# Sigmoid attention with a bilinear feed-forward: later start of the first group, thinner decoding, alternating banks for w3 and w_out

## The chip, the core and the metric

The kernel runs on one core of a Trainium2 chip. The metric is the device time of one execution in microseconds, as the median over several runs. The engines are named as in the profile: TensorE (PE, with PEld for its weight loads), VectorE (DVE), ScalarE (ACT), GpSimd (POOL) and SyncE (SP). SP and POOL here issue DMAs.

## What is computed

```python
def _attn_ref(q, k, v):                       # 8 batches, 12 heads, 448 tokens, head size 64
    scores = scale * np.matmul(q, k.transpose(0, 1, 3, 2)) - np.log(S)
    attn = 1.0 / (1.0 + np.exp(-scores))
    return np.matmul(attn, v).astype(np.float32)

def _moe_ref(x, w1, w2, w3, w_out):           # x: 3584 x 768, from the attention's output
    a = x @ w1                                # 768 x 1024
    b = x @ w2
    h = a * b @ w3                            # 1024 x 1024
    return (h @ w_out).astype(np.float32)     # 1024 x 768
```

The four weight matrices come as float64. The kernel gets them as pairs of 32-bit words and decodes them itself.

## The kernel before

**Arithmetic.** Every float32 operand of a large product is split into a high part (a cast to fp32r, mostly on ScalarE) and a low part (the operand minus its high part, on VectorE), and a product takes three matmuls: high x high, high x low, low x high. The large products are done by Strassen's method in Winograd's form: seven block products instead of eight, with names for the operands on the token side of `A11, S2, A12, S3, S1, A22, S4` (`PRODUCTS`). Product k takes one operand of each side. Sums of the products are formed on the way out of PSUM: product 0 is copied to `p` by ScalarE, product 1 gives `u2` = bank + p, product 3 `u3` = bank + p, product 2 is copied to `c11`, product 4 gives `c22`, products 5 and 6 finish. Products 1 and 3 share a PSUM bank, so do 0 and 2, and 4 and 6: the later of a pair goes on in the bank when the sum has been read out of it.

**Stages.** (1) Attention. The scores of a (batch, heads) tile are taken as `items`, 168 of them, in bursts of two or three (`sizes`); in each burst TensorE computes the burst's scores, ScalarE its sigmoids, and TensorE the products with v of the burst before (`attend_item`). A finished pair of heads is copied out of PSUM by ScalarE (`combine`) and becomes a block of x. (2) Four groups of two batches each: `up(g)` computes a * b for group g in eight rounds (`fc`, one column block of w1 and w2 each) of seven products of nine matmuls. It is a generator that yields after each matmul, and the callers deal it out by `take(filler, n)`. Group 0 is dealt out between the bursts of a window (bursts `WINDOW[0]` to `WINDOW[1]`, 36 matmuls after every second burst), groups 1 and 2 run as whole blocks behind one burst each (`blocks`), group 3 follows the last burst. (3) The product of w3 and w_out, made once (the w3 stage, 28 products of twelve matmuls, L870). (4) That product times a * b (L985), and the output.

**Work dealt out beside it.** All engines run in the order in which the program issues their instructions (for stage 3 and 4 that holds for TensorE and SyncE; the scheduler orders the others). So what a generator issues, and at which turn, sets the queues of VectorE and ScalarE:

- `change` (class `Units`) splits the token side's operands of the coming group, 21 units of a name and a block `kc`. An S2, S3 or S4 unit is a subtraction, a cast and a low part on VectorE; an A or S1 unit has its cast on ScalarE and its low part on VectorE. `__next__` issues the first unit of the list `left` whose inputs are there; `need(name)` issues what a product is about to read.
- `weights` (`prepare_weights`) decodes w1 and w2 and divides them into the seven operands of each column block. One step is one VectorE instruction of decoding or one operand divided (a ScalarE cast, a VectorE low part and a store by POOL). The steps are: one, then twelve of decoding for the first column block, then 23 for each next one, of which eleven divide the block before. Products of group 0 read these from SBUF (`ring`); if an operand isn't there, steps are taken until it is. Later groups load them from `w_dram` through SyncE, `RING - 1` = 5 products ahead (L421).
- `rest` (`prepare_rest`) decodes w3 and w_out after the window, 214 steps: six, then six for each of 32 jobs (L97, L103, L107, L112, L114, L118), and four sums for each quarter of w3. Its raw words are loaded through SyncE into four buffers (L85), its results are stored by POOL.
- `beside(g, n)` is called after each product of `up`: for group 0 it takes one unit and two steps of weights, for the others one unit or, when there is none, steps of `rest`.
- `pieces` (`split_wo`) runs beside group 3 from its second round on, one turn after each ten yields of `up`: it loads four blocks of one of four columns of w_out (POOL, `tw`), and makes the seven operands of that column, `th` and `tl`.

In the w3 stage `load_w3` brings an operand of w3 by SyncE into two buffers, `split_w3` makes its parts (three buffers), and `PLAN` says which product uses which bank and starts it anew.

Of the kernel before, what the change touches and what calls it, by code (L numbers as in the profile page):

```python
# [25 lines left out]
def sigmoid_attention_bilinear_ffn(  # L26
# [16 lines left out]
    nc = tc.nc  # L43
# [447 lines left out]
    def up(g):  # L491

        at = {b: slice(b * S, (b + 1) * S) for b in (2 * g, 2 * g + 1)}
        for fc in range(NF):
# [23 lines left out]
            for n in stream[(g * NF + fc) * 7:(g * NF + fc + 1) * 7]:  # L518
                share_upper("products")
                k = n % 7  # L520
                name = PRODUCTS[k]
                if g == 0:
                    while n not in ring:
                        next(weights)
                else:
                    load_weights(place[n] + RING - 1)
                w = ring.pop(n)
                bank, start, stop = ((0, 1, 0), (1, 1, 0), (0, 0, 1), (1, 0, 1),
                                     (2, 1, 0), (3, 1, 1), (2, 0, 1))[k]
                if start:  # L530
                    chain(bank)
                a = acc[bank]
                if fc == 0:
                    ahead = (2, 4, 4, 2 if n % 7 else 1)[g]
                    done = place[n] % (NF * 7)
                    first = stream[g * NF * 7:g * NF * 7 + 7]
                    for other in first[:done + ahead]:
                        change.need(PRODUCTS[other % 7])
                for kc in range(KH):
                    xh, xl = ops[g][name, kc]  # L540
                    for m, (i, x) in enumerate(((0, xh), (0, xl), (1, xh))):
                        nc.tensor.matmul(  # L542
                            a, w[:, i, kc], x, start=bool(start) and kc == 0 and m == 0,
                            stop=bool(stop) and kc == KH - 1 and m == 2, skip_group_check=True,
                        )
                        if (kc, m) != (KH - 1, 2):
                            yield
                used.add(n)
                if k == 0:
                    p = kept("p")  # L550
                    nc.scalar.copy(out=p, in_=a)  # L551
                elif k == 1:
                    u2 = kept("u2")
                    add(u2, a, p)
                elif k == 2:
                    c11 = kept("c11")
                    nc.scalar.copy(out=c11, in_=a)
                elif k == 3:
                    u3 = kept("u3")
                    add(u3, a, p)  # L560
                elif k == 4:
                    c22 = kept("c22")
                    add(c22, a, u3)
                elif k == 5:
                    add(u3, a, u3)
                    leave(2 * g + 1, u3, c22, u3)
                else:
                    add(u2, a, u2)
                    leave(2 * g, u2, c11, kept("c22"))
                beside(g, n)  # L570
                yield

# [25 lines left out]
    assert len(quad) == TILES  # L598
    items = [(t, x) for t in range(B * NQ) for x in quad]
    GROUP = NF * 7 * KH * 3  # L600
    sizes = [3] * 17 + [2] * 28 + [3] * 5 + [2] + [3] * 6 + [2] + [3] * 8
    WINDOW = (17, 45)
    blocks = {50: 1, 57: 2}
    NBURST = len(sizes)
    starts = [sum(sizes[:k]) for k in range(NBURST + 1)]
    bursts = [items[i:i + n] for i, n in zip(starts, sizes)] + [[]]
# [3 lines left out]
    def beside(g, n):  # L610

        if g == 0:
            take(change, 1)
            take(weights, 2)
        elif not take(change, 1):
            take(rest, 2)

    qks, splits, vvs = {}, {}, {}
    qks[0] = load_pair(0, (nc.sync, nc.scalar))
# [47 lines left out]
    for k in range(NBURST + 1):  # L667
# [13 lines left out]
                take(change, 3)  # L681
                take(weights, 3 if k < 9 else 2 if k < 13 else 1)
        elif not in_window and k not in blocks and k < NBURST:
            take(change, 4 if k < 50 else 3)
            take(rest, 1)
        now = []
        for i, (t, x) in enumerate(burst):
            if x is None:
# [12 lines left out]
        if k == WINDOW[0]:  # L701
            filler = up(0)
        if in_window:
            take(weights, 3)
            done = k + 1 - WINDOW[0]
            if done % 2 == 0:
                upto, since = (GROUP * i // (WINDOW[1] - WINDOW[0]) for i in (done, done - 2))
# [24 lines left out]
    def load_w3(n, queue=nc.sync):  # L732
        if n < NH * 7:
            w3f[n] = p3.tile([P, NH, P], F32, name="w3")
            queue.dma_start(out=w3f[n], in_=w3_dram[n])

    def split_w3(n):
        if n < NH * 7:
# [7 lines left out]
    def split_wo():  # L746
# [8 lines left out]

        for jc in range(NH):
            b11, b12, b21, b22 = load(jc)
            for _ in range(3):
                yield

            def put_wo(k, src):
                h, l = seven[k]
                split(h[:, jc], l[:, jc], src, nc.scalar.copy, nc.vector)

            for k, src in ((0, b11), (1, b21), (6, b22)):
                put_wo(k, src)
                yield
            t3 = temp()
            total(t3, b22, b12, ALU.subtract)
            put_wo(3, t3)  # L770
            yield
            total(b12, b12, b11, ALU.subtract)
            put_wo(4, b12)
            yield
            t2 = temp()
            total(t2, b22, b12, ALU.subtract)
            put_wo(2, t2)
            yield
            total(b21, b21, t2, ALU.subtract)
            put_wo(5, b21)  # L780
            yield

    pieces = split_wo()
    for n in range(2):
# [62 lines left out]
        h, l = stationary(which)  # L847
        split(h[:, ic], l[:, ic], src, nc.scalar.copy, nc.vector)

    PLAN = ((0, True), (0, False), (1, True), (1, False), (0, True), (1, False), (0, False))  # L850
    for ic in range(NH):
        bank = {}
        for k, (which, start) in enumerate(PLAN):
            n = ic * 7 + k
            split_w3(n + 2)
            load_w3(n + 4)
            if n in (7, 8):
# [162 lines left out]
```

## Time and profile before

| | |
|---|---|
| median of 3 runs | 995.9 us (995.31 to 996.9) |
| profiled execution | 996.26 us |
| its span in the profile | 994.5 us |
| mean granted TensorE clock | 0.996 |
| TensorE busy | 963.0 us, 97% of the span |
| VectorE busy | 700.5 us, 70% |
| ScalarE busy | 414.2 us, 42% |

The span is what lies between the first and the last instruction of the profiled execution. Busy is the sum of an engine's instructions. In a timeline a row is start, length, engine, line and operation; brackets hold the idle time of the engine before it and what ended that. Buffer numbers are left out of names, so `w` may be an operand of w1 and w2 or of w3.

### The profile page before, as it was taken

What the parts mean: (1) busy time and instruction counts of PE and PEld (TensorE: products, weight loads), DVE (VectorE), ACT (ScalarE), POOL (GpSimd) and SP (SyncE); (2) the same over time, 40 slices, a digit from 0 to 9 for tenths busy, and PEclk for the clock granted to TensorE, in tenths of its full rate; (3) what the DMA queues carried; (4) which work ended last, traced back from release to release, by engine and by line L of the source; (5) the groups of instructions that cost most, each with busy time, mean ns of one, the idle gap of its engine ahead of it and who ended that gap; (6) DMA issues with size and microseconds to landing.
All of it is one profiled execution on the core that took longest, in us unless ns stands there. A gap on an engine that the chain in (4) does not pass through costs nothing.

```text
span 994.5 us, 14280 instructions
## 1 busy us (share of the span) xinstructions
PE 963.0 (97%) x5190; PEld 747.7 (75%) x5190; DVE 700.5 (70%) x1153; ACT 414.2 (42%) x621; POOL 116.2 (12%) x204
## 2 busy tenths in 40 slices
PE   9999899999999999999999998999898999999998
PEld 4444566667665989847899746889788989999997
DVE  5769778887549878798788638455678687475653
ACT  6886456655557111283111462222255433323230
POOL 1110222321200112200212100211100000000000
PEclk9999999999999999999999999999999999999999
DMA  7765566776555899965999723888564324342402
GB/s 253 252 207 169 166 235 230 264 247 225 197 185 170 298 390 345 394 236 170 385 357 381 232 80 122 295 269 268 167 181 117 105 102 149 103 158 102 158 28 83
DMA packets 97605, 210.66 MB, mean 212 GB/s; under 512 B 10496, under 2 KB 57600, under 8 KB 97536
## 3 DMA queue, kind: packets, MB, share of 16 engines
q1 hardware_dynamic: 80880, 145.55, 44.3%
q0 software_dynamic: 16512, 63.98, 17.9%
q8 instruction: 41, 0.67, 0.3%
q14 instruction: 28, 0.23, 0.1%
q10 hardware_dynamic: 144, 0.23, 0.1%
HBM read 151.52 MB, written 58.20 MB: 211 GB/s over the span
## 4 chain that ended last, share of the span: by engine, by line
PE 73%; DVE 10%; DMA 9%; issue 5%; ACT 2%; POOL 1%; SPq 0%; ACTq 0%; POOLq 0%; DVEq 0%
PE up L542 28%; PE up L985 20%; PE av L219 10%; PE sp L196 7%; DMA w<-w_dram 5%; PE up L870 3%; PE av L227 2%; PE third L196 2%; DMA g_dram<-c 2%; PE sp L206 1%; DVE A L244 1%; DMA gf_b<-g_dram 1%; DVE lS L81 1%; DVE u L512 1%; DVE hS L80 1%
## 5 line engine op out<-in xcount | busy, mean ns | idle before, releaser
L542 PE MATMUL up<-hS,w 128*128 128x448 f32 x702 | 218.2, 370 | 11.4 <-DVE u L512 4.2
L542 PE MATMUL up<-hA,w 128*128 128x448 f32 x522 | 164.5, 369 | 0.8 <-ACT a L178 0.3
L542 PEld LDWEIGHTS up<-hS,w 128*128 128x128 f32 x702 | 132.2, 188 | 32.1 <-issue 7.7
L178 ACT ACTIVATE a<-sp,bias 128x896 f32<-128x896 f32 x132 | 129.6, 1011 | 49.2 <-PE sp L196 25.3
L542 PE MATMUL up<-lS,w 128*128 128x448 f32 x351 | 129.2, 368 | 0.4 <-DVE lS L81 0.4
L219 PE MATMUL av<-a,vv 128*64 128x448 f32 x576 | 124.8, 556 | 0.0
L985 PE MATMUL up<-gl,sh 128*128 128x448 f32 x336 | 123.3, 367 | 1.3 <-DVE gl L81 1.3
L985 PE MATMUL up<-gh,sh 128*128 128x448 f32 x336 | 123.3, 367 | 0.0
L985 PE MATMUL up<-gh,sl 128*128 128x448 f32 x336 | 123.3, 367 | 0.0
L542 PEld LDWEIGHTS up<-hA,w 128*128 128x128 f32 x522 | 98.4, 189 | 15.8 <-issue 4.2
L542 PE MATMUL up<-lA,w 128*128 128x448 f32 x261 | 95.7, 367 | 0.0
L551 ACT COPY p<-up 128x448 f32<-128x448 f32 x32 | 17.1, 534 | 174.1 <-PE up L542 149.5
L219 PEld LDWEIGHTS av<-a,vv 128*64 128x64 f32 x576 | 35.4, 137 | 66.1 <-issue 65.4
L512 DVE TENSOR_TENSOR u<-up,p 128x448 f32<-128x448 f32 x64 | 39.8, 623 | 55.4 <-PE up L542 55.2
L542 PEld LDWEIGHTS up<-lS,w 128*128 128x128 f32 x351 | 66.2, 188 | 6.7 <-DVE lS L81 1.4
L985 PEld LDWEIGHTS up<-gl,sh 128*128 128x128 f32 x336 | 63.1, 188 | 7.4 <-DVE gl L81 1.7
L985 PEld LDWEIGHTS up<-gh,sh 128*128 128x128 f32 x336 | 63.1, 188 | 5.8 <-ACT p L954 0.2
L985 PEld LDWEIGHTS up<-gh,sl 128*128 128x128 f32 x336 | 63.1, 188 | 5.7
L870 PE MATMUL up<-th,w3s 128*128 128x384 f32 x224 | 59.2, 338 | 7.0 <-ACT tw L876 3.0
L80 ACT CAST gh<-gf_b 128x896 fp32r<-128x896 f32 x40 | 35.7, 942 | 55.6 <-PE up L985 55.1
L196 PEld LDWEIGHTS sp<-high 64*128 64x128 f32 x226 | 21.4, 185 | 48.9 <-ACT a L178 37.8
L512 DVE TENSOR_TENSOR u<-up,u 128x448 f32<-128x448 f32 x64 | 39.8, 622 | 25.6 <-PE up L542 25.1
(107 smaller groups left out, 1579.8 us busy)
## 6 DMA issues: line engine op xcount, KB each, us to landing
w<-w_dram SPq DMA_DIRECT2D x168, 384.0 KB, 5.7
gf_b<-g_dram SPq DMA_DIRECT2D x16, 896.0 KB, 5.1
w_dram<-w POOLq DMA_DIRECT2D x36, 384.0 KB, 4.1
raw<-w POOLq DMA_DIRECT2D x16, 768.0 KB, 6.3
qk<-qT SPq DMA_DIRECT2D x48, 224.0 KB, 4.9
out<-o_sb SPq DMA_DIRECT2D x48, 224.0 KB, 1.9
qk<-kT SPq DMA_DIRECT2D x47, 224.0 KB, 5.0
vv<-vL SPq DMA_DIRECT2D x24, 384.0 KB, 3.7
```

Source lines behind the costliest of these rows:

```text
L80: hi_engine(out=dst_hi, in_=src)
L81: lo_engine.tensor_tensor(out=dst_lo, in0=src, in1=dst_hi, op=ALU.subtract)
L178: nc.scalar.activation(dst, src, AF.Sigmoid, bias=bias[:n], scale=scale)
L196: nc.tensor.matmul(sp[:, j], k[rows, 1, at:at + P], q[rows, 0], start=m == 0, stop=m == 2)
L206: nc.tensor.matmul(sp[HEADS[u], j], qk[rows, 1, FULL:], qk[rows, 0], start=True, stop=True)
L219: nc.tensor.matmul(acc[cols, :S], vv[:, c, at:at + D], a[:, j], start=u == 0 and c == 0, stop=u == 1 and c == NC - 2,)
L227: nc.tensor.matmul(acc[cols, :S], vs[HEADS[u], cols], a[HEADS[u], j], start=u == 1, stop=u == 0)
L512: nc.vector.tensor_tensor(out=out, in0=a, in1=b, op=ALU.add)
L542: nc.tensor.matmul(a, w[:, i, kc], x, start=bool(start) and kc == 0 and m == 0, stop=bool(stop) and kc == KH - 1 and m == 2, skip_group_ch ...
L551: nc.scalar.copy(out=p, in_=a)
L870: nc.tensor.matmul(acc, w[:, i, jc], t[:, jc], start=start and jc == 0 and m == 0, stop=jc == NH - 1 and m == 2, skip_group_check=True,)
L985: nc.tensor.matmul(acc, w[:, fc, ms], g[:, fc], start=start and fc == 0 and m == 0, stop=fc == NH - 1 and m == 2, skip_group_check=True,)
```

## The change

The window starts one burst later, behind 18 bursts of three instead of 17, and the first block too (burst 51); the burst that is added there is taken from those between the blocks. In the first two bursts of the window no steps of weights are taken. In the blocks `rest` gets two steps after two of three products and one after the third; in the bursts behind the second block it gets three steps instead of one. Group 3 looks one product ahead in its first four products, where it looked two ahead after the first. The w3 stage does its products in the order 0, 2, 1, 3, 4, 5, 6, and loads w3's operands in that order. In `split_wo` the high part is issued one turn before its low part, and a column takes nine turns instead of ten.

```diff
                 if fc == 0:
-                    ahead = (2, 4, 4, 2 if n % 7 else 1)[g]
                     done = place[n] % (NF * 7)
+                    ahead = (2, 4, 4, 2 if done > 3 else 1)[g]
                     first = stream[g * NF * 7:g * NF * 7 + 7]
                     for other in first[:done + ahead]:
                         change.need(PRODUCTS[other % 7])
...
-    sizes = [3] * 17 + [2] * 28 + [3] * 5 + [2] + [3] * 6 + [2] + [3] * 8
-    WINDOW = (17, 45)
-    blocks = {50: 1, 57: 2}
+    sizes = [3] * 18 + [2] * 28 + [3] * 5 + [2] + [3] * 5 + [2] + [3] * 8
+    WINDOW = (18, 46)
+    blocks = {51: 1, 57: 2}
...
         elif not take(change, 1):
-            take(rest, 2)
+            take(rest, 2 if n % 3 else 1)
...
         elif not in_window and k not in blocks and k < NBURST:
-            take(change, 4 if k < 50 else 3)
-            take(rest, 1)
+            take(change, 4 if k < 51 else 3)
+            take(rest, 1 if k < 57 else 3)
...
         if in_window:
-            take(weights, 3)
+            take(weights, 3 if k > WINDOW[0] + 1 else 0)
...
-            queue.dma_start(out=w3f[n], in_=w3_dram[n])
+            queue.dma_start(out=w3f[n], in_=w3_dram[(n // 7) * 7 + (0, 2, 1, 3, 4, 5, 6)[n % 7]])
...
             b11, b12, b21, b22 = load(jc)
-            for _ in range(3):
+            for _ in range(2):
                 yield
 
-            def put_wo(k, src):
+            def high_part(k, src):
+                nc.scalar.copy(out=seven[k][0][:, jc], in_=src)
+                return k, src
+
+            def low_part(k, src):
                 h, l = seven[k]
-                split(h[:, jc], l[:, jc], src, nc.scalar.copy, nc.vector)
-
-            for k, src in ((0, b11), (1, b21), (6, b22)):
-                put_wo(k, src)
+                nc.vector.tensor_tensor(out=l[:, jc], in0=src, in1=h[:, jc], op=ALU.subtract)
+
+            last = high_part(0, b11)
+            yield
+            for k, src in ((1, b21), (6, b22)):
+                following = high_part(k, src)
+                low_part(*last)
+                last = following
                 yield
-            t3 = temp()
-            total(t3, b22, b12, ALU.subtract)
-            put_wo(3, t3)
-            yield
-            total(b12, b12, b11, ALU.subtract)
-            put_wo(4, b12)
-            yield
-            t2 = temp()
-            total(t2, b22, b12, ALU.subtract)
-            put_wo(2, t2)
-            yield
-            total(b21, b21, t2, ALU.subtract)
-            put_wo(5, b21)
-            yield
+            t3, t2 = temp(), temp()
+            for k, out, in0, in1 in (
+                (3, t3, b22, b12), (4, b12, b12, b11), (2, t2, b22, b12), (5, b21, b21, t2)
+            ):
+                total(out, in0, in1, ALU.subtract)
+                following = high_part(k, out)
+                low_part(*last)
+                last = following
+                yield
+            low_part(*last)
...
-    PLAN = ((0, True), (0, False), (1, True), (1, False), (0, True), (1, False), (0, False))
+    PLAN = {0: (0, True), 2: (1, True), 1: (0, False), 3: (1, False),
+            4: (0, True), 5: (1, False), 6: (0, False)}
     for ic in range(NH):
         bank = {}
-        for k, (which, start) in enumerate(PLAN):
-            n = ic * 7 + k
+        for turn, (k, (which, start)) in enumerate(PLAN.items()):
+            n = ic * 7 + turn
```

## Rows read from the trace of the kernel before

**Rows 1.** The page, part 1: busy time, share of the span, instructions.
```profile
PE 963.0 (97%) x5190; PEld 747.7 (75%) x5190; DVE 700.5 (70%) x1153; ACT 414.2 (42%) x621; POOL 116.2 (12%) x204
```

**Rows 2.** Windows by stage: length, busy by engine, clock, DMA share, GB/s.
```profile
317.25:423.66 106.41, 103.59 (x506) 94.08 (x506) 86.26 (x167) 18.93 (x36) 19.97 (x37) 1.00 0.95 348
...
455.58:561.05 105.47, 104.33 (x508) 94.32 (x506) 80.52 (x155) 16.46 (x33) 20.00 (x37) 1.00 0.94 337
...
598.07:716.12 118.05, 110.60 (x517) 95.84 (x517) 72.40 (x132) 27.10 (x54) 18.71 (x35) 0.99 0.73 231
...
716.12:782.97 66.85, 60.63 (x337) 58.19 (x338) 47.06 (x83) 30.77 (x59) 0.85 (x2) 1.00 0.44 129
```

**Rows 3.** Chain of waits: start, length, line, matmuls; first block, w3 stage.
```profile
317.25 36.49 PE up L542 x180
...
724.29 10.59 PE up L870 x60
```

**Rows 4.** Timeline of TensorE, last group: start, length, [idle before, releaser].
```profile
606.66 0.37 PE L542 MATMUL up<-hS,w 128*128 128x448 f32 x1
...
609.17 0.47 PE L542 MATMUL up<-hS,w 128*128 128x448 f32 x1 [2.14 <-DVE u L512]
```

**Rows 5.** Timeline of TensorE at the start of the window.
```profile
100.08 0.47 PE L542 MATMUL up<-hS,w 128*128 128x448 f32 x1 [1.68 <-DVE u L512]
...
108.43 0.47 PE L196 MATMUL sp<-high 64*128 64x448 f32 x2 [3.16 <-ACT a L178]
```

**Rows 6.** Windows behind two gaps, columns as in rows 2.
```profile
109.30:113.40 4.10, 4.07 (x17) 1.49 (x15) 3.37 (x5) 4.10 (x7) 1.40 (x2) 0.58 0.32 107
...
631.50:635.00 3.50, 3.50 (x12) 3.13 (x11) 3.06 (x6) 0.66 (x2) 0.55 (x1) 0.53 0.40 155
```

**Rows 7.** Timeline of ScalarE at the start of the window.
```profile
105.10 0.51 ACT L80 CAST wo<-f 128x384 fp32r<-128x384 f32 x1 [6.14 <-DVE f L244]
```

**Rows 8.** Groups of VectorE, 92.65 to 317.25: busy, mean ns, idle before.
```profile
L107 DVE SCALAR_TENSOR_TENSOR f<-f,raw 128x768 uint32<-128x768 uint32 x12 | 11.4, 954 | 0.0
```

**Rows 9.** Timeline of TensorE, first block.
```profile
363.36 0.44 PE L542 MATMUL up<-hS,w 128*128 128x448 f32 x1 [2.14 <-DMA w<-w_dram]
```

**Rows 10.** DMA issues 340 to 366: size, us to landing.
```profile
w<-w_dram SPq DMA_DIRECT2D x13, 384.0 KB, 8.6
```

**Rows 11.** Waits of SyncE's queue, first block: total, times, longest.
```profile
SPq L85 <- DVE raw L97: 42.7, 13, 5.2
```

**Rows 12.** Timeline of VectorE, front of the second block.
```profile
454.91 0.62 DVE L244 TENSOR_TENSOR A<-A,A 128x448 f32<-128x448 f32 x1
...
459.61 0.62 DVE L512 TENSOR_TENSOR u<-up,p 128x448 f32<-128x448 f32 x1 [3.00 <-PE up L542]
```

**Rows 13.** Windows in the last bursts, columns as in rows 2.
```profile
570.00:580.00 10.00, 10.00 (x76) 4.81 (x72) 2.92 (x5) 7.35 (x10) 0.00 (x0) 1.00 0.46 139
```

**Rows 14.** Timeline of ScalarE, first round of the last group.
```profile
605.05 0.58 ACT L80 CAST hA<-A 128x448 fp32r<-128x448 f32 x1
```

**Rows 15.** Timelines of ScalarE (first row) and TensorE, last group.
```profile
629.27 0.51 ACT L80 CAST th<-tw 128x384 fp32r<-128x384 f32 x1 [5.03 <-DMA tw<-wo_dram]
...
630.96 0.47 PE L542 MATMUL up<-hS,w 128*128 128x448 f32 x1 [1.75 <-DVE c L512]
...
666.70 0.48 PE L542 MATMUL up<-hS,w 128*128 128x448 f32 x1 [0.21 <-DVE u L512]
...
699.44 0.47 PE L542 MATMUL up<-hS,w 128*128 128x448 f32 x1 [1.45 <-DVE c L512]
```

**Rows 16.** Timeline of ScalarE, third column of w_out.
```profile
669.59 0.51 ACT L80 CAST th<-tw 128x384 fp32r<-128x384 f32 x1 [2.47 <-DMA tw<-wo_dram]
```

**Rows 17.** Costliest groups, w3 stage: busy, mean ns, idle before by releaser.
```profile
L870 PE MATMUL up<-th,w3s 128*128 128x384 f32 x224 | 59.2, 338 | 7.0 <-ACT tw L876 3.0 <-DVE tw L244 1.7 <-ACT w3s L80 0.8
```

**Rows 18.** Timeline of ScalarE, first and last of six casts.
```profile
745.14 0.62 ACT L80 CAST w3s<-w 128x512 fp32r<-128x512 f32 x1 [2.93 <-DMA w<-w_dram]
...
766.43 0.62 ACT L80 CAST w3s<-w 128x512 fp32r<-128x512 f32 x1 [0.78 <-DMA w<-w_dram]
```

## Prediction

> **What bounds the kernel now.** I read the page first [rows 1]: TensorE is busy 963.0 of 994.5 us, so the time can only fall where TensorE stands idle, 31.5 us in all, and it rises where a new wait is made. The windows by stage [rows 2] say where the idle time lies; the reader takes PE busy from the length of each stretch. The first block (317.25 to 423.66) has 106.41 - 103.59 = 2.82, the second 1.14, the last group (598.07 to 716.12) 7.45, the w3 stage 6.22. With the two gaps at the start of the window [rows 5], 4.84, these 22.5 us are what the change can reach; nothing of it touches the matmuls themselves. Third, the timelines of TensorE for each gap, and of the engine named there for what stood ahead in its queue.
>
> A gap costs more than its bracket says. In a steady run 180 matmuls take 36.49, 0.203 a start [rows 3]. Around the gap of 2.14 the starts are 606.66 and 609.17 [rows 4]: 2.51 where one start takes 0.20, so 2.31 lost, 0.17 more than the bracket; and the matmul behind the gap has a row of 0.47 instead of 0.37. I add 0.27 for a gap removed.
>
> **First group a burst later.** Two gaps stand at the start of the window, 1.68 (for u on VectorE) and 3.16 (for a sigmoid) [rows 5]. Behind the second TensorE runs at 0.58 of its clock for 4.10 us [rows 6]: with x of it at 1.2 GHz, 1 - x/2 = 0.58, x = 0.84, so 3.4 us at half clock and 1.7 lost. The cause is a queue. ScalarE stood 6.14 us with a cast of wo at its head, which waited for a subtraction on VectorE [rows 7]; sigmoids were queued behind. VectorE was late since the three S4 units (three instructions each) were dealt among the first products, with three steps of weights per burst and two per product. The steps go: 1, then 12 for the first column block, then 23 for each next one (12 of decoding, 11 that divide the block before). Before, 34 are done when the window opens and 40 before its first product. After, burst 17 takes the three S4 units and one step (35), and the first two bursts of the window take none: 35 at the first product. So three units (nine instructions) and five steps leave the queue there, and the burst that takes them costs TensorE nothing new: its three tiles are only moved from behind the first block. I remove both gaps and the slow stretch: 1.68 + 3.16 + 2 x 0.27 + 1.7 = 7.1. Bounds: 0 (the same sigmoid stuck behind another cast) to 7.6 (a gap of 0.5 further on too).
>
> The clock part hangs on more than a gap's length: the gap of 2.14 at 609.17 was followed by full clock, the gap of 1.75 at 630.96 by 0.53 for 3.50 us [rows 6]. The Trainium skill ("TensorE: Matmul & The Clock Gate", "What's actually happening") says that the gate counts freely beside the kernel and half clock is the default that activity lifts. By it neither stretch is tied to its gap: the sum would be 1.7 us off to either side, should one stay or another appear. The rows agree as far as 2.14 without and 1.75 with a slow stretch go.
>
> **Decoding thinner in the blocks.** The blocks lose 2.82 + 1.14 = 3.96 in five gaps. The largest, 2.14, waits for a load of w [rows 9]. In that stretch a load of w takes 8.6 us [rows 10], and it is issued five products ahead, 5 x 9 x 0.203 = 9.1: next to no slack. And SyncE, which issues it, is held by loads of raw words that wait for VectorE to free a buffer: 42.7 us in 13 waits, up to 5.2 [rows 11]. The rest's 214 steps, counted: before, 5 in the bursts ahead of the first block, 110 in it (2 for each of 55 products, one product takes a unit), 6 between, and the last 93 in the second block. After, 5 + 91 + 5 + 89 = 190, and 8 x 3 = 24 in the last bursts: 214, none over. So both the raw loads and VectorE's steps thin by a sixth in the blocks. I take 4.0 of 3.96 + 5 x 0.27 = 5.3, as the DMA stays well filled. Bounds 0 to 5.3.
>
> What that moves. (a) Only five bursts, not six, lie between the blocks, with three units each, so the three S3 units (subtraction, cast and low part; the S4 unit that starts at 454.91 is over 3.00 ahead of 459.61, so 1.7 us [rows 12]) fall into the second block's front. There VectorE stands idle those 3.00 us for product 1 [rows 12], and the last burst's units are the three short A22 ones instead: cover enough, 0. (b) The last eight bursts get 24 steps, about 0.5 us each. VectorE is busy 2.92 of 10 us there [rows 13]; only the first burst behind the block is full, where the split of q and k has under 1 us to spare: +0.4. Bounds 0 to 1.0 for both.
>
> **Fewer units ahead in the last group.** Order there: A11, A12, S2, S3, S1, A22, S4. Before, S2 of the last kc is emitted ahead of A12's product. After, A12 needs nothing more, and what follows it is one unit off the list, A22 of that kc. Its cast is behind c11's copy on ScalarE, at 605.05 [rows 14], so its low part can't start before 605.65, and S2 (1.7 us) follows at 606.2 rather than 604.6. S2's product then ends near 608.5 instead of 607.0; u2 comes right behind and S3 starts near 609.2, as now (609.17). Nothing won, and the units behind stand one place later: S4's three end about 618.5 instead of 617.3, on which the seventh product waits: +1.2. Bounds -1.0 (the low part early, u2 directly behind S2's product) to +2.4.
>
> **Low parts of w_out a step behind; two yields, not three.** One column takes 9 turns of ten matmuls instead of 10. Before, high and low part go out together, so VectorE waits inside its queue for ScalarE's cast, which waits for the load. First column: cast at 629.27 after its load, c22 behind the low part, gap 1.75 at 630.96 [rows 15]. After, the first low part is emitted at the same place (turn 3, after four products), so this gap stays, slow clock with it: 0. Fourth column: gap 1.45 at 699.44 [rows 15]. Its loads go out at turn 27 instead of 30, ahead of the sixth round's stores, about 10 us sooner: gap gone, with three small ones (0.16, 0.22, and 0.21 at 666.70 [rows 15]) in which u or p was behind a cast: 1.45 + 0.59 + 4 x 0.27 = 3.1. Third column: its loads are pinned behind the round's stores, but its first low part comes at turn 21, after 3 products instead of 5. The load landed at 669.59 [rows 16]; cast, low part and u3, then the second cast and low part, then c22 follow one on the other at 0.5 to 0.6 each: about 672.5, where product 6 wants it at 671.5: +1.0. Net 2.1 won. Bounds 3.1 won to 1.0 lost.
>
> **Alternating banks in the w3 stage.** Before, product 1 continues the bank of product 0 and product 3 that of product 2 at once, so each waits for the read in between: eight gaps, the whole 6.22. One round of 60 matmuls without a gap takes 10.59, 0.174 each [rows 3]; a row is 0.338 [rows 17]; so each gap hides 0.25 more: 6.22 + 8 x 0.25 = 8.2. After, a product of 12 x 0.174 = 2.1 lies between write and read, against a copy of 0.5. What is late next: the loads of w3. Two buffers make a loop of cast, low part, load; five rounds of it took from 745.14 to 766.43 [rows 18], 4.26 each, and two products without gaps take 4.18. The splits run up to two products ahead, a lead of 4.18 less 1.4 = 2.8. VectorE's 47.06 busy in the stage [rows 2] become 80% of 58.6 us, so I take 4.5 a round: 13 x 0.32 - 2.8 = 1.4 of waits. Won: 6.8. Bounds 8.2 to 3.0.
>
> **Sum.** -7.1 - 4.0 + 0.4 + 1.2 - 2.1 - 6.8 = -18.4. The profiled execution took 996.26 (span 994.5 and 1.8 around it), 0.4 above the median of 995.9. 996.26 - 18.4 = 977.9; I say 978.0.
>
> **Rivals.** (1) The w3 loads become the bound: a round at 4.9, since the closing group of additions stands in VectorE's queue ahead of a low part; 13 x 0.72 - 2.8 = 6.6 of waits, 983. For it, the present 4.26; against, idle time on VectorE between products. (2) The sigmoid at the window's start stays stuck behind a divide: 7 comes back, 985. For it, two steps per product remain; against, the nine unit instructions are gone. (3) The last store of decoded w_out is issued in the last group's first round, shortly before w_out's first loads; if these wait for it to land (3 to 4 us), the gap at 630.96 grows: 981.5. Against: other rows of w_out. (4) The other side: the ring of weights runs dry as the window starts five steps back. A round whose block isn't decoded waits for two matrices of six instructions at up to 0.954 [rows 8], at most 2 x 5.7 = 11.4 us; one such round of seven gives 989, two 1001: from the second on it is slower. Against: product 8 needs step 49, and 35 + 16 + 12 = 63 are done by then. (5) The gaps only move, two of the three large terms coming back: 992 to 996.
>
> **How the numbers follow.** A measurement here tells 0.2% (2 us) from no change. The forecast (973 to 981.4) has 0.56, rival 1 0.14, rival 2 0.11, rival 3 0.08, rival 4 0.04, rival 5 0.05, better than 973 0.02. Up to 986 leaves out rivals 4 and 5 and part of 2; below I stop at 972.5, as all good bounds together give 971. Faster 0.91, same 0.05, slower 0.04.
>
> **What would show it.** Right: no gap over 0.5 in the first two rounds of the window, and full clock there; no wait for w in the first block; S2's product of the last group in its old place or later, with S4's low parts the wait; the gap for c22 in the second round still there, none in the sixth; the w3 stage 58 to 61 us long without a wait for tw. Wrong: a w3 stage above 63 with waits for w3s; a wait for a sigmoid near 105; waits for w in the window; splits late in the burst behind the second block.

## The result, and the profile after

The median goes from 995.61 us (992.67 to 996.9, 4 runs) to 983.51 us (981.69 to 986.56, 4 runs): ratio 0.9886, 95% interval 0.9849 to 0.9922, so 7.8 to 15.1 parts in a thousand less. The forecast of 978.0 was 5.5 us too low, and the time lies within its range of 972.5 to 986.0. The profiled execution of the change is the longest of its four, 986.56 us with a span of 984.8; against the span before, 994.5, that is 9.7 less, where the sum said 18.4.

Windows of the changed kernel by stage (length, then busy time of TensorE, its weight loads, VectorE, ScalarE and GpSimd, the granted clock, DMA share, GB/s): the two blocks, the last group, the w3 stage; then the start of the window, and three stretches at a lower clock.

```profile
313.47:416.51 103.04, 102.82 (x506) 94.44 (x504) 78.99 (x151) 17.29 (x33) 18.29 (x33) 1.00 0.93 331
443.47:545.91 102.44, 102.44 (x506) 94.52 (x504) 80.84 (x153) 17.29 (x34) 14.92 (x28) 1.00 0.94 336
...
584.08:707.98 123.90, 112.45 (x516) 98.05 (x517) 73.01 (x135) 27.09 (x54) 19.17 (x36) 0.96 0.70 222
707.98:773.09 65.11, 61.48 (x337) 59.67 (x338) 45.90 (x83) 30.97 (x59) 0.87 (x2) 0.97 0.43 131
92.00:112.00 20.00, 20.00 (x122) 12.53 (x115) 15.93 (x28) 11.85 (x17) 2.05 (x3) 1.00 0.59 188
596.00:600.00 4.00, 4.00 (x15) 3.57 (x15) 1.95 (x5) 0.00 (x0) 0.00 (x0) 0.66 0.26 91
623.00:630.00 7.00, 6.44 (x19) 5.75 (x20) 5.80 (x12) 2.05 (x4) 1.52 (x3) 0.54 0.38 123
731.00:737.00 6.00, 5.75 (x24) 5.79 (x25) 4.41 (x7) 2.40 (x3) 0.00 (x0) 0.72 0.93 308
```

Against [rows 2], the blocks are 3.37 and 3.03 shorter and hardly idle, the last group is 5.85 longer, and the w3 stage only 1.7 shorter. From 92 to 112 the window runs without a gap at full clock, where [rows 5] and [rows 6] had two gaps and 0.58. In return three stretches lose 4.0 x 0.34 + 7.0 x 0.46 + 6.0 x 0.28 = 6.3 us to the clock, where the two of [rows 6] lost 3.4.

The gaps are the second half of the reading. TensorE's timeline in the last group and the w3 stage (start, length, operation, in brackets the idle time before and what ended it):

```profile
593.54 0.47 PE L542 MATMUL up<-hS,w 128*128 128x448 f32 x1 [1.72 <-DVE hS L80]
...
595.59 0.74 PE L542 MATMUL up<-hS,w 128*128 128x448 f32 x1 [0.72 <-DVE u L512]
...
623.56 0.74 PE L542 MATMUL up<-hS,w 128*128 128x448 f32 x1 [5.13 <-DVE c L512]
666.27 0.47 PE L542 MATMUL up<-hS,w 128*128 128x448 f32 x1 [1.46 <-DVE c L512]
707.98 0.41 PE L875 MATMUL up<-th,w3s 128*128 128x384 f32 x1 [1.08 <-issue]
731.25 0.41 PE L875 MATMUL up<-th,w3s 128*128 128x384 f32 x1 [2.00 <-DVE tw L244]
747.24 0.62 PE L875 MATMUL up<-th,w3s 128*128 128x384 f32 x2 [1.04 <-DVE w3s L81]
```

The gap for c22, 1.75 before [rows 15], is 5.13. GpSimd's timeline and VectorE's show why. GpSimd:

```profile
608.68 0.54 POOL L488 DMA_DIRECT2D wo_dram<-f  x1
...
614.26 1.09 POOL L735 DMA_DIRECT2D w<-w_dram  x2 [4.39 <-DMA w<-w_dram]
615.35 2.15 POOL L753 DMA_DIRECT2D tw<-wo_dram  x4
```

VectorE:

```profile
622.41 0.56 DVE L767 TENSOR_TENSOR tl<-tw,th 128x384 fp32r<-128x384 f32 x1 [7.04 <-DMA tw<-wo_dram]
622.89 0.62 DVE L512 TENSOR_TENSOR c<-up,u 128x448 f32<-128x448 f32 x1
```

The last store of decoded w_out is issued at 608.68, between the two stores of the first round's output. The first loads of w3 stand behind it on GpSimd's queue and wait 4.39 us; w_out's four loads stand behind those. The bracket names a load of w as what came last; that the wait hangs on the store is what experiment 1 shows, and the time that the store took from issue to landing, 4.6 us, fits it:

```profile
wo_dram<-f POOLq DMA_DIRECT2D x1, 192.0 KB, 4.6
```

VectorE then waits 7.04 us for w_out at the head of its queue, and the addition for c22, for which TensorE waits, comes next.

### The profile page after: what moved, and what is told of

It is laid out like the page before. It is cut to its first block, busy times and chain, and to the rows that moved or that the text cites. A ratio compares the mean times of both kernels' runs of the same rounds, so it can differ in the third digit from the quotient of the medians.

```text
span 984.8 us, 14267 instructions
## 1 busy us (share of the span) xinstructions
PE 959.2 (97%) x5190; PEld 750.4 (76%) x5190; DVE 700.3 (71%) x1154; ACT 413.5 (42%) x620; POOL 115.8 (12%) x204
## 4 chain that ended last, share of the span: by engine, by line
PE 82%; DVE 8%; DMA 5%; issue 3%; ACT 1%; POOL 1%; SPq 0%; ACTq 0%; POOLq 0%; DVEq 0%
PE up L542 36%; PE up L990 20%; PE av L219 10%; PE sp L196 7%; PE up L875 4%; PE av L227 2%; PE third L196 1%; PE sp L206 1%; DMA tw<-wo_dram 1%; DMA w<-w_dram 1%; DVE A L244 1%; DVE lS L81 1%; DMA vv<-vL 1%; DMA g_dram<-c 1%; DMA gf_b<-g_dram 1%
## 5 line engine op out<-in xcount | busy, mean ns | idle before, releaser
L81 DVE TENSOR_TENSOR gl<-gf_b,gh 128x896 fp32r<-128x896 f32 x40 | 41.8, 1087 | 22.5 <-ACT gh L80 22.5
```

The source lines that it names most:

```text
L81: lo_engine.tensor_tensor(out=dst_lo, in0=src, in1=dst_hi, op=ALU.subtract)
```

## Experiments

Ratios are against the kernel before on the same chip, with 95% intervals. Since the same kernel's executions differ by some 7 us, the stages of one profile say more than a single time.

**1. The store ahead of the last group.**

```
         if k == NBURST:
+            take(rest, 10 ** 6)
             take(change, 4)
```

> The changed kernel with the end of the decoding (its last store, no instruction of VectorE) issued ahead of the last group instead of in its first round. Theory: the first loads of the w3 stage's operands wait for that store to land, so w_out's first loads come late; then GpSimd's wait of 4.39 us before these loads goes, the gap for c22 in the last group's second round falls from 5.13 to 2 or less, and the time falls by 3 to 6 us from 983.5. Rival: the loads are late since the first round ends late and the DMA is full; then the gap stays near 5 and the time within 1 us.

Measured: 982.98 us, ratio 0.9867 (0.9846 to 0.9888). GpSimd issues the store at 586.02, the wait ahead of w3's loads falls from 4.39 to 0.97, the gap for c22 from 5.13 to 0.21. The last group takes 118.95 instead of 123.90, although two stretches at half clock (596 to 600 and 606 to 610) remain in it. The store's place is the cause of the 5.13. The time, though, is only 0.5 us under the change's 983.51, not the 3 to 6 that were expected: of the 4.95 won in the last group, the w3 stage gives back 1.8 in this profile (66.87), with a stretch of 0.66 from 735 to 740.

**2. The old number of units ahead.**

```
-ahead = (2, 4, 4, 2 if done > 3 else 1)[g]
+ahead = (2, 4, 4, 2 if n % 7 else 1)[g]
```

> The changed kernel with the old look-ahead of the last group (two operands ahead after the first product). Theory of the prediction: the shorter look-ahead only puts S2 and S4 of the last block later; then the gap of 1.72 for hS goes, the gap for u grows from 0.72 to about 2, the waits for S4 shrink, the first round falls from 23.0 to 21.5 to 22, the time by 1 to 2 us. Rival: u2 being earlier is worth more than the later operands; then the round grows to 24 and the time rises by 1 or more.

Measured: 985.31 us, ratio 0.9895 (0.9872 to 0.9917). The first round takes 22.64 instead of 23.03, with gaps of 1.30 and 2.14 instead of 1.72 and 0.72, and the same clock (0.83, 0.50 and 0.82 in three successive stretches of 2 us). In the change this edit is worth 0.4 in the round, not the 1 to 1.5 expected, and nothing in the time. The gap for S2's operand, 1.72 before the edit and 1.30 after it, stays, since three steps of decoding of the last burst stand in VectorE's queue ahead of the last units. In the change's own profile:

```profile
584.52 0.36 DVE L112 TENSOR_SCALAR raw<-f 128x384 uint32<-128x384 uint32 x1
584.91 0.56 DVE L114 SCALAR_TENSOR_TENSOR raw<-raw 128x384 f32<-128x384 uint32 x1
585.50 0.56 DVE L118 TENSOR_TENSOR f<-f,raw 128x384 f32<-128x384 f32 x1
...
591.90 0.62 DVE L81 TENSOR_TENSOR lA<-A,hA 128x448 fp32r<-128x448 f32 x1
```

**3. Five steps of decoding in each of the last bursts, so that none is left over.**

```
-take(rest, 1 if k < 57 else 3)
+take(rest, 1 if k < 57 else 5)
```

> The changed kernel with five steps of decoding instead of three in each burst behind the second block, so that the decoding and its last store are over after five bursts. Theory: besides the wait for the store (as in the run with the store early) the last burst's three decoding instructions, 1.5 us, stand ahead of the last operands in VectorE's queue; then the last group's first round falls by 1.5 to 21.5 and the gap in its second round to 2 or less, the time by 5 to 8 us. Rival: VectorE is too full behind the block; then splits of q and k come late there and gaps of 1 to 3 us appear between the second block and the last group, and the time falls by less than with the store alone.

Measured: 979.06 us, ratio 0.983 (0.9809 to 0.9851). GpSimd's, VectorE's and TensorE's timelines of this run:

```profile
610.35 1.09 POOL L735 DMA_DIRECT2D w<-w_dram  x2 [0.98 <-DMA w<-w_dram]
611.44 2.15 POOL L753 DMA_DIRECT2D tw<-wo_dram  x4
```

```profile
592.59 0.62 DVE L81 TENSOR_TENSOR lA<-A,hA 128x448 fp32r<-128x448 f32 x1 [1.10 <-ACT hA L80]
```

```profile
594.23 0.47 PE L542 MATMUL up<-hS,w 128*128 128x448 f32 x1 [1.50 <-DVE hS L80]
...
596.28 0.48 PE L542 MATMUL up<-hS,w 128*128 128x448 f32 x1 [0.72 <-DVE u L512]
...
619.54 0.47 PE L542 MATMUL up<-hS,w 128*128 128x448 f32 x1 [1.84 <-DVE c L512]
```

The gap for c22 is 1.84, as the prediction wanted it, and the clock is full in the whole last group: 116.67 us instead of 123.90. The time is 4.5 us under the change's, a little less than the 5 to 8 expected. No decoding stands on VectorE ahead of the last units any more, yet the first round still takes 21.60 where the kernel before took 19.82: VectorE idles 1.10 us for A22's cast, which is behind c11's copy on ScalarE. Of the round's 3.2 us more in the change, 1.4 is the stretch at 0.66. The other 1.8 has two causes, of which either alone makes most of it: the gap for S2's operand is 1.72 with the decoding and the short look-ahead (the change), 1.30 with the decoding alone (experiment 2), 1.50 with the look-ahead alone (here), and it is gone without both (experiment 8).

**4. w3 straight into the low half of its split tile**, four tiles deep, so that a load waits for no low part.

```
-w3f[n] = p3.tile([P, NH, P], F32, name="w3")
+w3s[n] = p3.tile([P, 2, NH, P], F32R, name="w3s", bufs=4)
...
-load_w3(n + 4)
+if n:
+    load_w3(n + 3)
```

> The changed kernel with w3's operands loaded straight into four buffers of parts and split in place, so that a load waits for a product that is done and not for a split two operands back; the memory is the same. Theory: what took the place of the bank waits in the w3 stage is the loop of cast, low part and load, which holds ScalarE's queue; then the stage falls from 65.1 to 59 to 61 us and the time by 3 to 5. Rival: the closing group of additions on VectorE is what is late; then the stage stays at 63 or more and gaps for tw stay.

Measured: 983.89 us, ratio 0.9882 (0.9863 to 0.99). The w3 stage takes 61.30 instead of 65.11, with no stretch below full clock (the one at 0.72 is 1.7 of the 3.8); its largest gap inside is 0.56:

```profile
706.89:768.19 61.30, 59.83 (x337) 58.12 (x338) 45.39 (x82) 30.41 (x58) 0.55 (x1) 1.00 0.46 141
```

What this shows of the loop is read from the change itself, on ScalarE and VectorE:

```profile
725.40 0.62 ACT L80 CAST w3s<-w 128x512 fp32r<-128x512 f32 x1 [2.78 <-DMA w<-w_dram]
```

```profile
726.05 0.69 DVE L81 TENSOR_TENSOR w3s<-w,w3s 128x512 fp32r<-128x512 f32 x1 [1.78 <-ACT w3s L80]
726.66 0.55 DVE L244 TENSOR_TENSOR tw<-tw 128x384 f32<-128x384 f32 x1
...
730.55 0.55 DVE L244 TENSOR_TENSOR tw<-up,tw 128x384 f32<-128x384 f32 x1
```

A load is late, so its cast waits 2.78, so VectorE stands 1.78 for that cast in the middle of the closing group, and the addition at 730.55 that frees a bank comes last: the gap of 2.00 at 731.25. In this experiment that gap is 0.37. The size can't be taken from this pair alone: the unedited change took 61.85 in its second profile (experiment 9). Over all profiles the stage took 61.85 to 66.87 in the eight with the loop and the new banks, and 60.80 to 61.30 in the three without the loop (experiments 4, 8 and 12). The time here, 983.89, is the change's within what a measurement tells, against the 3 to 5 us expected; the last group holds the late store and three stretches at half clock still (122.95 us).

**5. The banks alone, on the kernel before** (the new PLAN and the new order of loads).

> The kernel before with the alternating banks and the matching load order alone. Theory (the loads of w3 and VectorE's closing group take the place of the eight bank gaps): the w3 stage goes from 66.85 us to about 65, with gaps of 1 to 2 us for tw or w3s in place of the eight for the banks; 1.5 to 2 us in all, about 993.8. Rival (the banks were worth what the prediction took, 6.8, and something else of the whole change spoils the stage): the stage is about 60, the time about 989.

Measured: 992.05 us against 994.26, ratio 0.9981 (0.9966 to 0.9996). Window and gaps of its w3 stage:

```profile
712.91:779.29 66.38, 60.55 (x336) 57.94 (x337) 45.93 (x83) 30.94 (x59) 0.88 (x2) 1.00 0.42 130
```

```profile
736.18 0.41 PE L871 MATMUL up<-th,w3s 128*128 128x384 f32 x1 [2.00 <-DVE tw L244]
744.01 0.44 PE L871 MATMUL up<-th,w3s 128*128 128x384 f32 x1 [1.32 <-ACT w3s L80]
752.38 0.62 PE L871 MATMUL up<-th,w3s 128*128 128x384 f32 x2 [1.09 <-DVE w3s L81]
```

At full clock the stage takes 66.38, where the same cut (first product to first product of the next stage) gives 66.70 before: the eight gaps for the banks went, five for loads and VectorE came. In this profile the part gave 0.3 us in the stage, less than the 1.5 to 2 expected. By time it gave 2.2, with an interval of 0.4 to 3.4; what the profile has less ahead of the stage, the edit doesn't touch.

**6. The window alone, on the kernel before** (sizes, WINDOW, blocks, no weights in two bursts).

> The kernel before with the first group a burst later alone (sizes, window, blocks, no weights in the first two bursts of the window). Theory (VectorE's late units kept a cast and so a sigmoid back): no gap over 0.3 us in the first two rounds of the window, full clock there, 7.1 to 7.6 us less: about 988. Rival (the first gaps need the thinner decoding too, or come back in the blocks, since one burst less lies between them): 4 us or less, 991.5 or more.

Measured: 987.14 us, ratio 0.994 (0.9919 to 0.9961). From 92 to 110 us TensorE is busy throughout, at full clock:

```profile
92.00:110.00 18.00, 18.00 (x108) 11.05 (x106) 16.55 (x28) 10.34 (x15) 2.05 (x3) 1.00 0.57 178
```

Up to the first block and between the blocks, cut as in the table below, the profile is 7.0 shorter than before. The two parts of the edit, the burst more and the steps of weights left out, were not tried apart. The blocks still wait for w, 1.90 and 0.71, and take 104.47 and 103.29: 4.1 together less than [rows 2], though their decoding is the old one. Whether that came with the window or differs from execution to execution, one profile doesn't tell.

**7. The thin decoding alone, on the kernel before** (one or two steps per product in the blocks, three per burst in the last eight).

> The kernel before with the decoding thinned alone (two steps or one per product in the blocks, three per burst in the last eight). Theory: the two blocks lose their five gaps, 6.4 us; the last group's first round is about 1 us longer, as three decoding instructions stand ahead of the last units; there are six bursts between the blocks, one step more than in the whole change, so the last store of decoded w_out is issued ahead of the last group, and the wait for c22 in its second round is 2 us or less: about 990.5. Rival (the thinner decoding makes that wait grow to 5 us, however the store stands): about 994.

Measured: 989.77 us, ratio 0.9962 (0.9948 to 0.9976). Both blocks without a gap:

```profile
316.34:418.68 102.34, 102.34 (x506) 94.60 (x505) 78.67 (x149) 17.29 (x33) 18.29 (x34) 1.00 0.93 334
449.76:552.12 102.36, 102.36 (x507) 94.50 (x505) 77.91 (x148) 17.21 (x34) 17.07 (x32) 1.00 0.95 341
```

That is 7.2 less than [rows 2], 4.1 and 3.1. Six bursts lie between the blocks here, one step more than in the change, and the store goes out at 591.83 and not after the first round; the gap for c22 is 2.39. So one step decides on the 5.13. The last group's start pays as in the change: a gap of 0.93 for a late unit, then 2.14, then a lower clock from 602 to 608. By time the parts of experiments 5 to 7 sum to 11.7 us (1.9, 6.0 and 3.8 by their ratios), the whole change, with the look-ahead and the low parts, to 11.4.

**8. Three edits together:** 3, 2 and 4.

> The changed kernel with three edits together: five steps of decoding per burst in the last eight (nothing left over for the last group), the old number of units ahead in the last group's first round, and w3 loaded straight into the low half of its split tile. Theory, from the profile of the run with five steps alone (span 978.1): first round 21.6 to 19.8, as before (-1.8), w3 stage 64.9 to 61.3 (-3.5): span 972.8, 974.6 in all, ratio about 0.979. Rival (the units ahead are worth nothing here, and VectorE fills up in the w3 stage all the same): 978 to 979.

Measured: 976.51 us, ratio 0.9839 (0.9816 to 0.9862), span 974.5. The w3 stage takes 60.80, the first round 21.06, of which some 1.7 is a stretch at half clock behind a gap of 2.15. That stretch is what the 974.6 of the expectation left out: without it the round is at 19.4, against 19.8 before.

**9. The change again**, beside the next two.

> The changed kernel as it is, as a measure for the two beside it: 983 to 985 us, with a wait for c22 of 4.5 to 5.5 us in the last group's second round and half clock behind it.

Measured: 984.85 us (980.54 to 987.93), ratio 0.9916 (0.9895 to 0.9936). Its profile has a span of 978.8, 6.0 less than the first one. Of that, 3.1 lie in the last group (120.77), where c22's gap is 1.50 and not the 4.5 to 5.5 expected: TensorE came to it 3.0 us later, after two stretches at half clock, and w_out's first low part 0.7 sooner. The store landed after 2.9 us here, and the wait of w3's loads was 2.73 (the bracket names a matmul, again what came last by the profile):

```profile
614.23 1.09 POOL L735 DMA_DIRECT2D w<-w_dram  x2 [2.73 <-PE up L542]
```

Another 3.3 lie in the w3 stage. VectorE's wait in the midst of the closing group, 1.78 in experiment 4's rows, is 0.64 here, the gap of 2.00 is 0.93 (727.26), and no stretch is below full clock:

```profile
705.28:767.13 61.85, 59.49 (x337) 58.02 (x337) 45.91 (x83) 31.13 (x59) 0.87 (x2) 1.00 0.43 136
```

```profile
722.07 0.69 DVE L81 TENSOR_TENSOR w3s<-w,w3s 128x512 fp32r<-128x512 f32 x1 [0.64 <-ACT w3s L80]
```

So the stage differs by 3.3 us between two executions of one kernel, 1.7 of it the clock, the rest what the late loads cost.

**10. Experiment 3 with the old low parts of w_out** (high and low part together, three turns of waiting).

> The changed kernel with five steps of decoding per burst in the last eight (the store of decoded w_out out of the way), and with the old splitting of w_out: high and low part of a block together, three turns of waiting and not two. Theory (the low parts a step behind are worth the 3.2 us by which rounds 2 to 8 were shorter than before, 95.1 for 98.2): rounds 2 to 8 take about 98, the gap of the fourth column comes back at 0.8 to 1.5, that of the third column goes, and the time is 981 to 982 in place of 979. Rival (that difference is only the stretch at half clock which before had behind its c22 gap): rounds 2 to 8 take 95 to 96.5, and the time is 979 to 980.

Measured: 983.01 us, ratio 0.9893 (0.9876 to 0.9909). The gap of the third column is gone and that of the fourth back with 1.29 (688.50). The gap for c22 in the second round is gone as well: TensorE came to it later, behind a first round of 24.1 us. Rounds 2 to 8 take 96.46 with 1.7 us lost to the clock from 608 to 612, most of it inside them, against 95.07 at full clock in experiment 3. Of what the span is longer, 4.3 us, 2.5 lie in the first round, which the edit doesn't touch. Windows of 594 to 602 and 608 to 612, first of this run, then of experiment 3:

```profile
594.00:602.00 8.00, 7.09 (x20) 5.65 (x21) 3.80 (x7) 0.00 (x0) 0.00 (x0) 0.57 0.29 86
608.00:612.00 4.00, 3.86 (x11) 3.45 (x12) 2.40 (x5) 0.00 (x0) 1.08 (x2) 0.57 0.47 160
```

```profile
594.00:602.00 8.00, 6.87 (x30) 5.32 (x30) 5.57 (x11) 0.00 (x0) 0.00 (x0) 1.00 0.34 106
608.00:612.00 4.00, 4.00 (x21) 3.71 (x20) 1.04 (x2) 0.53 (x1) 2.35 (x6) 1.00 0.82 243
```

**11. Experiment 3 again.**

> The kernel with five steps of decoding per burst in the last eight, once more, beside the kernel before on another chip. Theory (the store of decoded w_out is worth 4 to 6 us, and the old low parts 2 or more): ratio 0.982 to 0.985, as the first time. Rival (the first time only the stretches at half clock stayed out, which the same gaps brought in other kernels): a profile with half clock in the last group's first round, ratio 0.987 to 0.989, as with the old low parts, which are then worth nothing.

Measured: 981.45 us (977.61 to 983.78), ratio 0.9865 (0.9839 to 0.989). Its profile is again at full clock in the last group (116.58 us, c22's gap 1.75); among its six executions those with a mean clock of 0.999 and 1.000 took 977.61 and 978.04, those with 0.993 to 0.998 took 981.04 to 983.78. In experiment 3 time and clock did not go together: the fastest of its four, 976.48, had the lowest clock, 0.996, and 979.89 had 1.000. Neither expectation is met whole: the store's gain holds, and how much of the difference between 0.983 and 0.9865 is the clock stays open. Over both runs, 10 executions, the median is 979.9; that of the change (experiment 9 and the first four), 10 executions too, 984.3.

**12. Experiments 3 and 4 with w_out's first loads ahead of w3's.**

```
-    for n in range(2):
-        load_w3(n, nc.gpsimd)
     ...
         take(pieces, 1)
+        if turn == 0:
+            for n in range(2):
+                load_w3(n, nc.gpsimd)
```

> Five steps of decoding per burst in the last eight, w3 loaded straight into its split tile, and the first four loads of w_out issued ahead of the first two of w3 on GpSimd's queue; the units ahead as in the change. Theory (the two loads of w3, 1.09 us of issue, stand ahead of w_out's): the wait for c22 in the second round falls from 1.8 to 0.8, the w3 stage takes 61.3, and the span is 978.1 - 1.0 - 3.5 = 973.6, the time about 975, ratio 0.979 to 0.981. Rival (the loads of w_out take their time from the bytes ahead of them, not from the order of issue, and a stretch at half clock eats the rest): the wait stays near 1.8, the time is 976.5 or more.

Measured: 977.13 us, ratio 0.9834 (0.9817 to 0.985). The gap for c22 is gone, the w3 stage takes 61.22; three stretches at half clock in the last group (120.14 us) eat the difference. It doesn't beat experiment 8 by anything that can be told.

## Why the prediction came out as it did

Worked from the profiled executions (the head of the program, which the change doesn't touch, was 1.1 shorter after; it is left out of the first term, which adds the stretch from the first gap at 81.52 to the first block and that between the blocks, 267.65 before and 260.05 after):

| Term | Predicted | In the change | Alone |
|---|---|---|---|
| first group a burst later | -7.1 | -7.6 | -7.0 (experiment 6; by time -6.0) |
| blocks | -4.0 | -6.4 | -7.2 (experiment 7) |
| bursts behind the second block | +0.4 | +1.2 | |
| first round of the last group | +1.2 | +3.2 | +1.8 at full clock without the decoding (experiment 3) |
| rounds 2 to 8 | -2.1 | +2.6 | -3.2 without the late store (experiment 3), 1.7 of it a slow stretch that only before had |
| w3 stage, cut as in experiment 5 | -6.8 | -1.6 | -0.3 (experiment 5, one profile) |
| head, final stage | 0 | -1.1 | |

**Window: right**, mechanism and size. The cast of wo that stood 6.14 us ahead of the sigmoids [rows 7] now goes without a wait, and the sigmoid behind it waits for its scores alone:

```profile
102.51 0.52 ACT L80 CAST wo<-f 128x384 fp32r<-128x384 f32 x1
104.78 1.98 ACT L178 ACTIVATE a<-sp,bias 128x896 f32<-128x896 f32 x2 [1.75 <-PE sp L196]
```

**Blocks: right in kind, mis-sized.** The removed gaps were priced at their brackets and 0.27 each, 5.3 at most; a block without gaps takes 102.35, so the two lost 7.2. The other 1.9 has no bracket. Some 1.4 of it was a slower pace: behind its last gap the second block before ran 324 matmuls in 67.18, 0.207 a start and not 0.203, at a granted clock of 1.00. No run here shows why.

```profile
493.93 67.18 PE up L542 x324
```

The rows to price a starved stretch by are its length against the pace of a clean one: 504 matmuls at 0.203 [rows 3] give 102.3, and the two lengths of [rows 2] would have given 7.3.

**Bursts behind the second block: mis-sized.** They took 1.2 more where 0.4 was forecast and 1.0 was the bound. The sign that was named for it, a late split in the first burst there, is in the profile, with a gap of 0.56 at 551.12.

**Look-ahead: right mechanism, but not the only one.** A22's cast behind c11's copy, and VectorE idle for it, stand in experiment 3's profile with 1.10 where 1.2 of delay was forecast; the round lost 1.8. In the change itself VectorE comes to A22's low part without a wait (591.90, experiment 2), since the last burst's three steps of decoding have made it late already. The prediction counted these steps in their burst and not in the queue ahead of the last group. In the change the gaps are also followed by 1.4 at half clock, which the prediction left at full clock after one gap of 2.14.

**w_out: the step that failed is the count of the decoding.** "214, none over": 214 steps end in 214 stops of the generator, but the last store stands behind the last stop and needs a 215th. With 190 + 24 taken, it was emitted after the first round. Rival 3 then happened, by a way it had not named: not w_out's rows, but the first w3 tiles ahead of w_out's loads in GpSimd's queue. Its price of 3 to 4 us of wait compares with 4.39, and c22's gap grew by 3.4, with 1.6 more at half clock behind it. Experiments 1, 3 and 7 take it back with the store. The gap itself, at 1.84 without the store, stayed as forecast, and the third column's gap came as forecast (1.46 for 1.0). What the low parts a step behind are worth by themselves stays open: 0.9893 in experiment 10 is above the interval of experiment 3, but overlaps with that of its second run, 0.9839 to 0.989, and the profile puts more than half of the difference into a stretch that the edit doesn't touch. In rounds 2 to 8 the lower clock of experiment 10 cost 1.7, and the c22 gap that it lacks, 1.84 in experiment 3, about makes up for that.

**w3 banks: the step that failed is the loop of loads.** 4.5 us a round and a lead of 2.8 made 1.4 of waits. Experiment 5 has 5.6 in five gaps, with their 0.25 each 6.9, against the 6.6 of rival 1: that rival described the stage, with its mechanism, the closing group and the low part on one queue. The 80% of VectorE that the prediction weighed was the wrong measure; the order of its queue decides, since it stood idle 1.78 in the midst of the closing group. With the slow stretches taken out, the eight profiles with this loop won 0.3 to 4.9 us against 66.70, six of them less than the lower bound of 3.0. Without the loop the three profiles take 60.80 to 61.30, at the edge of the 58 to 61 that the prediction named.

So two rivals happened, and the range held all the same, by luck in part: the blocks gave 2.4 more than forecast, and the median lies 3 us under the profiled execution. The forecast was not right for its own sum: by the sum it missed 8.7 in the profile.

## What to carry to other kernels

Count what a generator still has to do behind its last stop, and look up what is queued behind a store or load that slips by one step. Price a starved stretch by its length against a clean one, not by its gaps. When a step of decoding is moved, look up what is queued behind it in the next stage too. When waits for banks or buffers are removed from a stage, look through the queue of the engine that takes over, in order, for an instruction that waits for a transfer: its busy share says little.

## What was not expected of the hardware

**The clock does not follow from a gap.** Experiments 3 and 10 have the same gaps at the start of the last group, 1.50 and 0.72; from 594 to 602 the one is granted 1.00, the other 0.57, that is 2.4 GHz against 1.2 for most of the stretch. The change, with 1.72 and 0.72 both times, got 0.66 from 596 to 600 in one execution and 0.57 over twice that time in the other. The prediction's 1.7 for a stretch that goes with its gap held where it was taken away, but stretches that cost 1.4 to 3.4 us come and go between executions of one kernel. In experiment 11 the spread of 6 us went with the clock, in experiment 3 the spread of 3.5 did not, so the clock isn't shown to be all of it. The Trainium skill ("TensorE: Matmul & The Clock Gate", "What's actually happening") has the gate count freely beside the kernel; the two runs with equal gaps and unequal clock agree with that.

**A slower TensorE can hide a late load:** in experiment 9, where 5.1 us were lost to the clock from 594 to 602 and 608 to 612, the same late store left a gap of 1.50 for c22 instead of 5.13: TensorE came to it 3.0 us later, and w_out's low part 0.7 sooner.
